# A six-layer cross network on one core: transposing loads in halves, a table for the last biases, and a different split of the first evictions

## The chip, the cores and the metric

The kernel runs on one core of one Trainium2 chip. The metric is the time of one execution on the device in microseconds (us). Three timed runs of the kernel before gave 131.05 us as median, 130.94 as lowest and 131.28 as highest.

## The reference

`x0` is a 4096 x 416 matrix, `ws` holds six 416 x 416 weight matrices and `bs` six bias rows of 416, all in bf16.

```python
def reference(x0, ws, bs):
    x = x0
    for l in range(ws.shape[0]):
        x = x0 * (x @ ws[l] + bs[l]) + x
    return x
```

Each layer is one matrix product over the width, a bias, an elementwise product with `x0` and a sum. In layer 0 `x` is `x0`, so the kernel computes `x0 * (x0 @ ws[0] + bs[0] + 1)` and adds the 1 to the bias beforehand.

## The kernel before, in words

**Layout.** In layers 0 to 4 the activations lie transposed: the width on the 128 partitions, the 4096 rows along the free dimension. The 416 columns are three blocks of 128 (`XM`, blocks `m` or `k`) and a remainder of 32 (`XR`). The rows are two halves `s` of 2048, and each half is four column groups `g` of 512 (`CW`). In the last layer the roles of weights and activations are exchanged, so that its results come out row by row and can be stored as they are.

**Loads.** `load_x0t` (L76) is a DMA that transposes on the way: 512 rows by 384 columns of `x0` go to the three blocks of one column group of `XM[0]`. There are eight. Their order is written out by hand on the queue of SyncE (SP): group 0 at L95, group 1 at L110, `xrem` at L111, groups 2 to 5 at L112 to L115, `xrem` of the second half at L116, groups 6 and 7, then the weights of layer 1 (`load_wm`, L119), the weight rows of the remainder (`load_wr`, L121), the other weights, `X0rows` and a row of last biases, `bLr` (L125). The first weights, the biases and the first weight rows come over the queue of ScalarE (ACT) (L96 to L98), and so does one `xrem` (L275). `xrem` is the 32-column remainder of `x0`, fetched in 64-byte pieces and turned by `x0_rem` (L153): VectorE (DVE) transposes of 32 x 32 blocks, a copy into `XR`, and a copy `XRx` with its halves exchanged.

**Start.** While the first loads are under way TensorE (PE) multiplies a constant tile (`pe_filler`, L148 to L150): three matmuls of 128 columns, nine of 512 and one of 256.

**First layer** (`first_layer`, L226). For each half `s` there are two parts `h` of two column groups. In a part, `full` (L229) issues three matmuls of 512 columns for a block and a column group, 18 in all for the part. In part 0 of half 0 they go group by group: three blocks on group 0, then three on group 1. In half 1 the order is block 0 and 1 on the first group of the part, block 0 and 1 on the second, then block 2 on both, so that the third step already needs the second group. Then `row` (L235) adds the remainder's 32 rows, and the results leave PSUM. `split_first` (L175) empties a block with two engines: ACT takes the first bank with the bias, and DVE the second bank with bias and product in one instruction. `ew_main` (L163) lets ACT take both banks, and DVE multiplies. PSUM is four pairs of banks, handed out in the order of `first_order` (L135): the second block of the next part takes the pair of block 0, and the third takes the pair of block 2.

**Middle layers** (L300). Each of the six tiles (`s`, `m`) of a layer takes 48 matmuls of 32 output rows (L197) and four row matmuls (L203); ACT adds the bias (L166), and DVE multiplies and adds (L171, L172). The results of layer 4 are turned back into rows by DMAs (`xl_dmat` L221, and `scrR` L284 with a POOL copy).

**Last layer** (L329 on). The eight `quads` hold four 128-row pieces each. `mm_q_rows` (L347) multiplies the remainder's rows (L351) and adds the biases by a matmul of one row of ones with a row of `bLr` (L356). `ew_pair` (L360) copies two pieces from PSUM (ACT), multiplies, adds (DVE) and stores on SP. The last two quads go piece by piece (`ew_single`, L371): the sum and store of a piece (`close`) are issued one piece later, after the next piece's product.

Of the kernel before, what the change touches and what calls it, by code (L numbers as in the profile page):

```python
# [9 lines left out]
ACT = mybir.ActivationFunctionType  # L10
ALU = mybir.AluOpType
BF16 = mybir.dt.bfloat16
# [4 lines left out]
def kernel(  # L17
# [16 lines left out]
    CW = 512  # L34
    SW = NG * CW
    NBT = B // P
    LL = L - 1
# [11 lines left out]

    dz = const.tile([P, 2], FP32)  # L50
    warm = const.tile([P, CW], BF16)
    ones = const.tile([P, P], BF16)
    WM = const.tile([P, L, NK, D], BF16)
    WR = const.tile([P, L, D], BF16)
    WD = const.tile([P, L, NG, R], BF16)
    bsb = const.tile([R, D], BF16)
    bT = const.tile([R, D // R, R], BF16)
    bLr = const.tile([P, D], BF16)
# [11 lines left out]
    def col0(s, g):  # L70
        return SW * s + CW * g

    def load_wm(eng, l):
        eng.dma_start(WM[:, l], ws[l, 0:NK * P, :].rearrange("(k p) n -> p k n", p=P))

    def load_x0t(s, g):  # L76
        c0 = col0(s, g)
        nc.sync.dma_start_transpose(out=XM[0][:, :, c0:c0 + CW], in_=x0[c0:c0 + CW, 0:NK * P])


    def load_xrem(eng, s, p0, p1):
# [9 lines left out]
    nc.gpsimd.memset(bsb[:], 0.0)  # L91
    nc.gpsimd.memset(ones[:], 1.0)
    nc.gpsimd.memset(WD[:], 0.0)

    load_x0t(0, 0)  # L95
# [5 lines left out]
    nc.vector.transpose(out=bT[:], in_=bsb.rearrange("p (c r) -> p c r", r=R))  # L101
    for q in range(4):
        nc.gpsimd.tensor_copy(bM[32 * q:32 * q + 32, :, :], bT[:, q:4 * NK:4, 0:L])
    nc.gpsimd.tensor_scalar(out=bM[:, :, 0:1], in0=bM[:, :, 0:1], scalar1=1.0, scalar2=None, op0=ALU.add)
# [1 line left out]
        nc.gpsimd.tensor_copy(bR[32 * g:32 * g + 32, :], bT[:, 4 * NK, 0:L])  # L106
    nc.gpsimd.tensor_scalar(out=bR[:, 0:1], in0=bR[:, 0:1], scalar1=1.0, scalar2=None, op0=ALU.add)
    for g in range(1, NG):
        nc.vector.tensor_copy(WR[32 * g:32 * g + 32, 0, :], WR[0:32, 0, :])
    load_x0t(0, 1)  # L110
    load_xrem(nc.sync, 0, 0, 64)  # L111
    load_x0t(0, 2)  # L112
    load_x0t(0, 3)
    load_x0t(1, 0)
    load_x0t(1, 1)  # L115
    load_xrem(nc.sync, 1, 0, 128)  # L116
    load_x0t(1, 2)
    load_x0t(1, 3)
    load_wm(nc.sync, 1)  # L119
    for g in range(NG):  # L120
        load_wr(nc.sync, g, 1, L)  # L121
    for l in range(2, L):
        load_wm(nc.sync, l)
    nc.sync.dma_start(X0rows[:], x0_v)
    nc.sync.dma_start(bLr[0:P:32, :], bs[LL:LL + 1, :].broadcast_to([NG, D]))  # L125

    def fill_wd(l0, l1):
        for g in range(NG):
# [15 lines left out]
    def pe_filler(n, cols):  # L144
        for i in range(n):
            nc.tensor.matmul(PS[:, 0, 0:cols], lhsT=warm[:, 0:P], rhs=warm[:, 0:cols], start=True, stop=True, skip_group_check=True)  # L146

    pe_filler(3, P)  # L148
    pe_filler(9, CW)
    pe_filler(1, 2 * P)  # L150


    def x0_rem(s, p0, p1, parts):  # L153
# [6 lines left out]
            nc.vector.tensor_copy(XRx[s][64 - a:128 - a, :], XR[0][a:a + 64, CW * s:CW * s + CW])  # L160


    def ew_main(l, s, m, h, pt, cur, nxt):  # L163
        c0 = col0(s, 2 * h)
        t = tpool.tile([P, 2 * CW], BF16, name="t")
        nc.scalar.activation(t[:], pt.rearrange("p a b -> p (a b)"), ACT.Identity, bias=bM[:, m, l:l + 1], scale=1.0)  # L166
        x0c = XM[0][:, m, c0:c0 + 2 * CW]
        if l == 0:
            nc.vector.tensor_tensor(out=nxt[:, m, c0:c0 + 2 * CW], in0=t[:], in1=x0c, op=ALU.mult)  # L169
            return  # L170
        nc.vector.tensor_tensor(out=t[:], in0=t[:], in1=x0c, op=ALU.mult)  # L171
        nc.vector.tensor_tensor(out=nxt[:, m, c0:c0 + 2 * CW], in0=t[:], in1=cur[:, m, c0:c0 + 2 * CW], op=ALU.add)  # L172


    def split_first(s, m, h, pt, nxt):  # L175
        c0 = col0(s, 2 * h)
        t = tpool.tile([P, 2 * CW], BF16, name="t")
        nc.scalar.activation(t[:, 0:CW], pt[:, 0, :], ACT.Identity, bias=bM[:, m, 0:1], scale=1.0)  # L178
        nc.vector.scalar_tensor_tensor(out=nxt[:, m, c0 + CW:c0 + 2 * CW], in0=pt[:, 1, :], scalar=bM[:, m, 0:1],
                                       in1=XM[0][:, m, c0 + CW:c0 + 2 * CW], op0=ALU.add, op1=ALU.mult)  # L180
        nc.vector.tensor_tensor(out=nxt[:, m, c0:c0 + CW], in0=t[:, 0:CW], in1=XM[0][:, m, c0:c0 + CW], op=ALU.mult)

    def ew_rem(l, s, pr, curR, nxtR):
        tr = tpool.tile([P, 2 * CW], BF16, name="t")
# [41 lines left out]
    def first_layer(s):  # L226
        cur, nxt = XM[0], XM[1]

        def full(pt, m, h, gl, first, last):  # L229
            c0 = col0(s, 2 * h + gl)  # L230
            for k in range(NK):
                nc.tensor.matmul(pt[:, gl, :], lhsT=WM[:, 0, k, 128 * m:128 * m + 128], rhs=cur[:, k, c0:c0 + CW],  # L232
                                 start=(first and k == 0), stop=(last and k == NK - 1), skip_group_check=True)
# [9 lines left out]
        for m, gl in ((0, 0), (1, 0), (2, 0), (0, 1), (1, 1), (2, 1)) if s == 0 else ((0, 0), (1, 0), (0, 1), (1, 1), (2, 0), (2, 1)):  # L243
            full(pa[m], m, 0, gl, True, False)
        pb = [two_banks()]
        row(pa[0], 0, 0, 0, False)
        if s == 1:
            row(pb[0], 0, 1, 0, True)
        row(pa[2], 2, 0, 0, False)
        row(pa[1], 1, 0, 1, False)  # L250
        split_first(s, 0, 0, pa[0], nxt)
        if s == 0:
            x0_rem(0, 64, 128, (nc.vector.tensor_copy,))
        for m in (2, 1):
            ew_main(0, s, m, 0, pa[m], cur, nxt)
        pb += [two_banks() for m in range(1, NK)]
        for m, gl in ((0, 0), (1, 0), (2, 0), (0, 1), (1, 1), (2, 1)) if s == 0 else ((0, 0), (1, 0), (0, 1), (1, 1), (2, 0), (2, 1)):
            full(pb[m], m, 1, gl, s == 0 or m > 0, s == 1 and m == 0)
            if s == 1 and (m, gl) == (0, 1):
                ew_main(0, s, 0, 1, pb[0], cur, nxt)  # L260
        if s == 0:
            row(pb[0], 0, 1, 0, False)
            row(pb[1], 1, 1, 0, False)
            row(pb[2], 2, 1, 1, False)
            split_first(s, 0, 1, pb[0], nxt)
            x0_rem(1, 0, 128, (nc.vector.tensor_copy,))
            for m in range(1, NK):
                ew_main(0, s, m, 1, pb[m], cur, nxt)
        else:
            row(pb[1], 1, 1, 0, False)  # L270
            row(pb[2], 2, 1, 1, False)
            rem_first(pb)

    x0_rem(0, 0, 64, (nc.scalar.copy, nc.vector.tensor_copy))
    load_xrem(nc.scalar, 0, 64, 128)  # L275

    def rem_pair(l, cur, curR, nxtR, feeds_last):
        pr2 = two_banks()
# [50 lines left out]
    l = LL  # L329
# [17 lines left out]
    def mm_q_rows(qs, pys, begun):  # L347
        for q, py in zip(qs, pys):
            s, i = quads[q]
            for g in range(NG):  # L350
                nc.tensor.matmul(py[g // 2][:, g % 2, 0:D], lhsT=curR[32 * g:32 * g + 32, CW * s + 128 * i:CW * s + 128 * i + 128],  # L351
                                 rhs=WR[32 * g:32 * g + 32, l, :], start=not (q == begun and g < 2), stop=False,
                                 tile_position=(32 * g, 0), skip_group_check=True)
        for q, py in zip(qs, pys):
            for g in range(NG):
                nc.tensor.matmul(py[g // 2][:, g % 2, 0:D], lhsT=ones[32 * g:32 * g + 1, :],  # L356
                                 rhs=bLr[32 * g:32 * g + 1, :], start=False, stop=(q == begun and g < 2), tile_position=(32 * g, 0),
                                 skip_group_check=True)

    def ew_pair(q, h, py):  # L360
# [4 lines left out]
        o = opool.tile([P, 2, D], BF16, name="o")  # L365
        nc.scalar.copy(tv, py[h][:, :, 0:D])  # L366
        nc.vector.tensor_tensor(out=tv, in0=tv, in1=X0rows[:, b0:b0 + 5:4, :], op=ALU.mult)  # L367
        nc.vector.tensor_tensor(out=o[:], in0=tv, in1=XLrows[:, b0:b0 + 5:4, :], op=ALU.add)  # L368
        nc.sync.dma_start(out_v[:, b0:b0 + 5:4, :], o[:])

    def ew_single(q, g, py):  # L371
        s, i = quads[q]
# [64 lines left out]
```

## Time and profile before

One profiled execution took 130.53 us. Its span, from the first to the last instruction, is 128.7 us; 1.8 us lie around it.

| | before |
|---|---|
| median of three timed runs | 131.05 us |
| profiled execution | 130.53 us |
| its span | 128.7 us |
| PE busy | 122.9 us (95%) |
| DVE busy | 104.2 us (81%) |
| ACT busy | 83.3 us (65%) |
| share of PE in the chain that ended last | 93% |
| the eight `x0` transposing loads, issue to landing | 4.3 to 5.8 us, median 4.8 |

The page gives busy time of each engine first, then the span in 40 slices, the DMA queues, the chain of work that ended last (each instruction followed back to what released it), and the costliest groups of instructions. A row "SPq" is the time in which SP was busy issuing a DMA; the transfer and its landing come later. "PEld" is the load of weights into the array; with back-to-back matmuls its starts show the pace of PE.

### The profile page before, as it was taken

Reading aid. Unit: us, or ns where it says so; the run is one execution under the profiler, and the core shown is the slowest. Engines: PE = TensorE matmul, PEld = TensorE weight load, DVE = VectorE, ACT = ScalarE, POOL = GpSimd, SP = SyncE. Lnnn points to the kernel's source line nnn. Section 1 sums busy time; section 2 is a strip of 40 time slices with the busy share of each in tenths; the row PEclk is TensorE's granted clock in tenths of the full one; section 3 lists DMA queues with packets and bytes.
Section 4 is the critical chain, followed back from the end, with each engine's and each line's share of the span. In section 5 each row is a group of like instructions: output and inputs, shape, how many; then the busy total and the mean of one; then the engine's idle time right before and its main releaser. Section 6 shows DMA issues by size and latency. Waiting matters only on the chain.

```text
span 128.7 us, 3923 instructions
## 1 busy us (share of the span) xinstructions
PE 122.9 (95%) x1677; PEld 54.5 (42%) x1677; DVE 104.2 (81%) x187; ACT 83.3 (65%) x93; POOL 7.0 (5%) x27
## 2 busy tenths in 40 slices
PE   6999999999999999999999999999999999999950
PEld 3343334444434444544444444434444445544420
DVE  1344969457979898989898989898989999999990
ACT  2117358399757759766749666849666877567760
POOL 4250000030000000000000000000000300000000
PEclk9999999999999999999999999999999999999999
DMA  3989989999991000000000000000398899995663
GB/s 94 261 155 222 179 153 277 225 326 333 335 316 30 5 0 8 0 0 5 0 5 0 5 0 5 0 0 5 73 135 185 163 150 234 235 293 176 198 192 103
DMA packets 41973, 16.37 MB, mean 127 GB/s; under 512 B 30778, under 2 KB 41956, under 8 KB 41956
## 3 DMA queue, kind: packets, MB, share of 16 engines
q1 hardware_dynamic: 40456, 15.70, 54.8%
q10 hardware_dynamic: 1500, 0.42, 1.6%
q8 instruction: 13, 0.21, 0.7%
q14 instruction: 4, 0.03, 0.1%
HBM read 6.15 MB, written 3.41 MB: 74 GB/s over the span
## 4 chain that ended last, share of the span: by engine, by line
PE 93%; ACT 2%; DVE 2%; issue 1%; DVEq 0%; ACTq 0%
PE PS L197 49%; PE PS L342 12%; PE PS L232 12%; PE PS L203 5%; PE PS L214 5%; PE PS L146 4%; PE PS L209 2%; PE PS L351 2%; PE PS L239 1%; PE PS L356 1%; DVE t L377 1%; ACT t L166 1%; DVE o L380 1%; ACT t L178 1%; ACT t L376 0%
## 5 line engine op out<-in xcount | busy, mean ns | idle before, releaser
L166 ACT ACTIVATE t<-PS,bM 128x1024 bf16<-128x1024 f32 x57 | 59.1, 1115 | 21.2 <-PE PS L203 21.2
L197 PE MATMUL PS<-XM,WM 128*32 128x512 bf16 x1152 | 65.2, 379 | 0.0
L197 PEld LDWEIGHTS <-WM 128*32 128x32 bf16 x1152 | 29.8, 97 | 33.7 <-issue 5.1
L171 DVE TENSOR_TENSOR t<-t,XM 128x1024 bf16<-128x1024 bf16 x48 | 33.3, 694 | 4.2 <-ACT t L166 4.2
L172 DVE TENSOR_TENSOR XM<-t,XM 128x1024 bf16<-128x1024 bf16 x48 | 33.5, 698 | 3.1
L342 PE MATMUL PS<-WM,XM 128*128 128x416 bf16 x96 | 17.9, 340 | 0.0
L232 PE MATMUL PS<-XM,WM 128*128 128x512 bf16 x72 | 16.9, 385 | 0.2 <-ACT t L166 0.2
L366 ACT CAST t<-PS 128x832 bf16<-128x832 f32 x12 | 10.2, 852 | 5.0 <-PE PS L342 2.3
L342 PEld LDWEIGHTS <-XM 128*128 128x128 bf16 x96 | 8.9, 98 | 8.7 <-issue 2.2
L232 PEld LDWEIGHTS <-WM 128*128 128x128 bf16 x72 | 6.9, 99 | 10.1 <-issue 2.8
L214 PE MATMUL PS<-XM,WM 128*32 128x512 bf16 x120 | 8.2, 379 | 0.0
L185 ACT ACTIVATE t<-PS,bR 128x512 bf16<-128x512 f32 x10 | 6.8, 694 | 2.0 <-POOL WD L129 2.0
L368 DVE TENSOR_TENSOR o<-t,XLrows 128x832 bf16<-128x832 bf16 x12 | 7.1, 592 | 0.5
L203 PE MATMUL PS<-XR,WR 32*128 32x512 bf16 x96 | 7.3, 379 | 0.0
L169 DVE TENSOR_TENSOR XM<-t,XM 128x1024 bf16<-128x1024 bf16 x9 | 5.9, 688 | 1.5 <-ACT t L166 1.5
L367 DVE TENSOR_TENSOR t<-t,X0rows 128x832 bf16<-128x832 bf16 x12 | 7.0, 584 | 0.0
L146 PE MATMUL PS<-warm 128*128 128x512 bf16 (+2 forms) x13 | 4.6, 535 | 1.0 <-DVE warm L88 1.0
L178 ACT ACTIVATE t<-PS,bM 128x512 bf16<-128x512 f32 x3 | 2.1, 687 | 5.3 <-PE PS L239 5.3
L285 POOL COPY XLrows<-scrR 128x512 bf16<-128x512 bf16 x2 | 1.3, 666 | 72.7 <-DMA scrR<-XR 72.7
L157 DVE STREAM_TRANSPOSE xrt<-xrem 64x256 bf16<-64x256 bf16 (+2 forms) x4 | 2.2, 562 | 3.5 <-DMA xrem<-in_x_dram 3.5
L376 ACT CAST t<-PS 128x416 bf16<-128x416 f32 x8 | 4.0, 506 | 1.0 <-PE PS L342 0.8
L214 PEld LDWEIGHTS <-WM 128*32 128x32 bf16 x120 | 3.2, 97 | 3.2
(40 smaller groups left out, 48.1 us busy)
## 6 DMA issues: line engine op xcount, KB each, us to landing
X0rows<-in_x_dram SPq DMA_DIRECT2D x1, 3328.0 KB, 15.3
out_dram<-o SPq DMA_DIRECT2D x12, 208.0 KB, 2.6
WM<-in_ws_dram SPq DMA_DIRECT2D x5, 312.0 KB, 6.5
out_dram<-o SPq DMA_DIRECT2D x8, 104.0 KB, 1.7
WR<-in_ws_dram SPq DMA_DIRECT2D x4, 130.0 KB, 6.0
WM<-in_ws_dram ACTq DMA_DIRECT2D x1, 312.0 KB
XM<-in_x_dram SPq DMA_TRANSPOSE x8, 4.8
xrem<-in_x_dram SPq DMA_DIRECT2D x1, 128.0 KB, 4.4
```

The source lines that it names most:

```text
L146: nc.tensor.matmul(PS[:, 0, 0:cols], lhsT=warm[:, 0:P], rhs=warm[:, 0:cols], start=True, stop=True, skip_group_check=True)
L166: nc.scalar.activation(t[:], pt.rearrange("p a b -> p (a b)"), ACT.Identity, bias=bM[:, m, l:l + 1], scale=1.0)
L171: nc.vector.tensor_tensor(out=t[:], in0=t[:], in1=x0c, op=ALU.mult)
L172: nc.vector.tensor_tensor(out=nxt[:, m, c0:c0 + 2 * CW], in0=t[:], in1=cur[:, m, c0:c0 + 2 * CW], op=ALU.add)
L197: nc.tensor.matmul(pts[g // 2][32 * q:32 * q + 32, g % 2, :], lhsT=WM[:, l, k, 128 * m + 32 * q:128 * m + 32 * q + 32], rhs=cur[:, k, c0:c ...
L203: nc.tensor.matmul(pts[g // 2][:, g % 2, :], lhsT=WR[32 * g:32 * g + 32, l, 128 * m:128 * m + 128], rhs=curR[32 * g:32 * g + 32, CW * s:CW ...
L214: nc.tensor.matmul(pr[32 * g:32 * g + 32, :], lhsT=WM[:, l, k, NK * P:D], rhs=cur[:, k, c0:c0 + CW], start=False, stop=(k == NK - 1), tile ...
L232: nc.tensor.matmul(pt[:, gl, :], lhsT=WM[:, 0, k, 128 * m:128 * m + 128], rhs=cur[:, k, c0:c0 + CW], start=(first and k == 0), stop=(last ...
L342: nc.tensor.matmul(py[g // 2][:, g % 2, 0:D], lhsT=cur[:, k, q_cols(q, g)], rhs=WM[:, l, k, :], start=(first and k == 0), stop=((not first ...
L366: nc.scalar.copy(tv, py[h][:, :, 0:D])
L367: nc.vector.tensor_tensor(out=tv, in0=tv, in1=X0rows[:, b0:b0 + 5:4, :], op=ALU.mult)
L368: nc.vector.tensor_tensor(out=o[:], in0=tv, in1=XLrows[:, b0:b0 + 5:4, :], op=ALU.add)
```

## The change

1. `load_x0t` fetches 256 rows, so there are sixteen loads in place of eight. On SP's queue the two halves of a group follow each other. The `xrem` that went over ACT's queue is now on SP's, behind group 3. `bLr` and its load are gone.
2. PE's fillers are three of 128 columns, seven of 512 and one of 128.
3. The first column group of half 0 is multiplied in two halves of 256 columns: nine matmuls on the first, nine on the second.
4. In part 0 of half 0, blocks 0 and 2 are both emptied by `split_first`; block 1 is copied by ACT. The DVE products of the first banks are issued after both splits, and that of block 1 after the turning of `xrem`, whose copy is shared between ACT and DVE.
5. The last biases come from `bsb`, whose rows 0 to 5 are the six biases; POOL copies them to the other three groups of 32 partitions. `pick[1]` has ones in row 5 of each group of 32, so a matmul with K = 32 picks the last bias.
6. The first four quads of the last layer collect four pieces in `o4` and store them with one DMA each; at the end, the sums of some pieces are issued earlier (`keep`).

```diff
-    def load_x0t(s, g):
-        c0 = col0(s, g)
-        nc.sync.dma_start_transpose(out=XM[0][:, :, c0:c0 + CW], in_=x0[c0:c0 + CW, 0:NK * P])
+    def load_x0t(s, g, a):
+        c0 = col0(s, g) + HW * a
+        nc.sync.dma_start_transpose(out=XM[0][:, :, c0:c0 + HW], in_=x0[c0:c0 + HW, 0:NK * P])
...
-    nc.gpsimd.memset(ones[:], 1.0)
+    nc.vector.memset(pick[0][:], 0.0)
+    nc.vector.memset(pick[0][:, LL:P:R], 1.0)
+    nc.vector.transpose(out=pick[1][:], in_=pick[0][:])
...
+    for g in range(1, NG):
+        nc.gpsimd.tensor_copy(bsb[32 * g:32 * g + 32, :], bsb[0:R, :])
...
-    load_x0t(0, 1)
+    load_x0t(0, 0, 1)
+    load_x0t(0, 1, 0)
+    load_x0t(0, 1, 1)
     load_xrem(nc.sync, 0, 0, 64)
-    load_x0t(0, 2)
-    load_x0t(0, 3)
-    load_x0t(1, 0)
-    load_x0t(1, 1)
+    load_x0t(0, 2, 0)
+    load_x0t(0, 2, 1)
+    load_x0t(0, 3, 0)
+    load_x0t(0, 3, 1)
+    load_xrem(nc.sync, 0, 64, 128)
+    load_x0t(1, 0, 0)
...
-    nc.sync.dma_start(bLr[0:P:32, :], bs[LL:LL + 1, :].broadcast_to([NG, D]))
...
-    pe_filler(9, CW)
-    pe_filler(1, 2 * P)
+    pe_filler(7, CW)
+    pe_filler(1, P)
...
+        if s == 0:
+            for part in range(2):
+                for m in range(NK):
+                    full(pa[m], m, 0, 0, True, False, part)
...
-        split_first(s, 0, 0, pa[0], nxt)
         if s == 0:
-            x0_rem(0, 64, 128, (nc.vector.tensor_copy,))
-        for m in (2, 1):
-            ew_main(0, s, m, 0, pa[m], cur, nxt)
+            closing = [split_first(s, 0, 0, pa[0], nxt)]
+            closing.append(split_first(s, 2, 0, pa[2], nxt))
+            t1 = ew_copy(0, 1, pa[1])
+            for close in closing:
+                close()
+            x0_rem(0, 64, 128, (nc.scalar.copy, nc.vector.tensor_copy))
+            nc.vector.tensor_tensor(out=nxt[:, 1, 0:2 * CW], in0=t1, in1=XM[0][:, 1, 0:2 * CW], op=ALU.mult)
...
-    load_xrem(nc.scalar, 0, 64, 128)
...
-                nc.tensor.matmul(py[g // 2][:, g % 2, 0:D], lhsT=ones[32 * g:32 * g + 1, :],
-                                 rhs=bLr[32 * g:32 * g + 1, :], start=False, stop=(q == begun and g < 2), tile_position=(32 * g, 0),
+                nc.tensor.matmul(py[g // 2][:, g % 2, 0:D], lhsT=pick[1][32 * g:32 * g + 32, :],
+                                 rhs=bsb[32 * g:32 * g + 32, :], start=False, stop=(q == begun and g < 2), tile_position=(32 * g, 0),
...
+        if q >= 4:
+            nc.sync.dma_start(out_v[:, b0:b0 + 5:4, :], o)
+        elif h == 1:
+            nc.sync.dma_start(out_v[:, b0 - 8:b0 + 5:4, :], o4[q][:])
...
-            close = ew_single(q, g, py)
-            if pending:
-                pending.pop()()
-            pending.append(close)
-    pending.pop()()
+            pending.append(ew_single(q, g, py))
+            keep = 0 if (q, g) in ((NQ - 2, NG - 1), (NQ - 1, 0), (NQ - 1, NG - 1)) else 1
+            while len(pending) > keep:
+                pending.pop(0)()
```

More of the change, by code (lines that the diff above doesn't have):

```diff
@@ L34 @@
     CW = 512
+    HW = CW // 2
     SW = NG * CW
@@ L51 @@
     warm = const.tile([P, CW], BF16)
-    ones = const.tile([P, P], BF16)
+    pick = [const.tile([P, P], BF16, name=f"pick{i}") for i in range(2)]
     WM = const.tile([P, L, NK, D], BF16)
@@ L55 @@
     WD = const.tile([P, L, NG, R], BF16)
-    bsb = const.tile([R, D], BF16)
+    bsb = const.tile([P, D], BF16)
     bT = const.tile([R, D // R, R], BF16)
-    bLr = const.tile([P, D], BF16)
     bM = const.tile([P, NK, L], FP32)
@@ L90 @@
     nc.vector.memset(dz[:], 0.0)
-    nc.gpsimd.memset(bsb[:], 0.0)
-    nc.gpsimd.memset(ones[:], 1.0)
+    nc.gpsimd.memset(bsb[0:R, :], 0.0)
+    nc.vector.memset(pick[0][:], 0.0)
+    nc.vector.memset(pick[0][:, LL:P:R], 1.0)
+    nc.vector.transpose(out=pick[1][:], in_=pick[0][:])
     nc.gpsimd.memset(WD[:], 0.0)
-    load_x0t(0, 0)
+    load_x0t(0, 0, 0)
     load_wm(nc.scalar, 0)
@@ L99 @@
     nc.scalar.activation(dz[:, 1:2], dz[:, 0:1], ACT.Identity, bias=dz[:, 0:1], scale=1.0)
-    nc.vector.transpose(out=bT[:], in_=bsb.rearrange("p (c r) -> p c r", r=R))
+    nc.vector.transpose(out=bT[:], in_=bsb[0:R, :].rearrange("p (c r) -> p c r", r=R))
     for q in range(4):
@@ L108 @@
     for g in range(1, NG):
+        nc.gpsimd.tensor_copy(bsb[32 * g:32 * g + 32, :], bsb[0:R, :])
+    for g in range(1, NG):
         nc.vector.tensor_copy(WR[32 * g:32 * g + 32, 0, :], WR[0:32, 0, :])
-    load_x0t(0, 1)
+    load_x0t(0, 0, 1)
+    load_x0t(0, 1, 0)
+    load_x0t(0, 1, 1)
     load_xrem(nc.sync, 0, 0, 64)
-    load_x0t(0, 2)
-    load_x0t(0, 3)
-    load_x0t(1, 0)
-    load_x0t(1, 1)
+    load_x0t(0, 2, 0)
[4 more added lines that the diff above has]
+    load_x0t(1, 0, 0)
+    load_x0t(1, 0, 1)
+    load_x0t(1, 1, 0)
+    load_x0t(1, 1, 1)
     load_xrem(nc.sync, 1, 0, 128)
-    load_x0t(1, 2)
-    load_x0t(1, 3)
+    load_x0t(1, 2, 0)
+    load_x0t(1, 2, 1)
+    load_x0t(1, 3, 0)
+    load_x0t(1, 3, 1)
     load_wm(nc.sync, 1)
@@ L160, in x0_rem, with ew_copy @@
             nc.vector.tensor_copy(XRx[s][64 - a:128 - a, :], XR[0][a:a + 64, CW * s:CW * s + CW])
+    def ew_copy(l, m, pt):
+        t = tpool.tile([P, 2 * CW], BF16, name="t")
+        nc.scalar.activation(t[:], pt.rearrange("p a b -> p (a b)"), ACT.Identity, bias=bM[:, m, l:l + 1], scale=1.0)
+        return t[:]
     def ew_main(l, s, m, h, pt, cur, nxt):
         c0 = col0(s, 2 * h)
-        t = tpool.tile([P, 2 * CW], BF16, name="t")
-        nc.scalar.activation(t[:], pt.rearrange("p a b -> p (a b)"), ACT.Identity, bias=bM[:, m, l:l + 1], scale=1.0)
+        t = ew_copy(l, m, pt)
         x0c = XM[0][:, m, c0:c0 + 2 * CW]
         if l == 0:
-            nc.vector.tensor_tensor(out=nxt[:, m, c0:c0 + 2 * CW], in0=t[:], in1=x0c, op=ALU.mult)
+            nc.vector.tensor_tensor(out=nxt[:, m, c0:c0 + 2 * CW], in0=t, in1=x0c, op=ALU.mult)
             return
-        nc.vector.tensor_tensor(out=t[:], in0=t[:], in1=x0c, op=ALU.mult)
-        nc.vector.tensor_tensor(out=nxt[:, m, c0:c0 + 2 * CW], in0=t[:], in1=cur[:, m, c0:c0 + 2 * CW], op=ALU.add)
+        nc.vector.tensor_tensor(out=t, in0=t, in1=x0c, op=ALU.mult)
+        nc.vector.tensor_tensor(out=nxt[:, m, c0:c0 + 2 * CW], in0=t, in1=cur[:, m, c0:c0 + 2 * CW], op=ALU.add)
     def split_first(s, m, h, pt, nxt):
@@ L180, in split_first @@
                                        in1=XM[0][:, m, c0 + CW:c0 + 2 * CW], op0=ALU.add, op1=ALU.mult)
-        nc.vector.tensor_tensor(out=nxt[:, m, c0:c0 + CW], in0=t[:, 0:CW], in1=XM[0][:, m, c0:c0 + CW], op=ALU.mult)
+        return lambda: nc.vector.tensor_tensor(out=nxt[:, m, c0:c0 + CW], in0=t[:, 0:CW], in1=XM[0][:, m, c0:c0 + CW], op=ALU.mult)
     def ew_rem(l, s, pr, curR, nxtR):
@@ L227, in first_layer, with full @@
         cur, nxt = XM[0], XM[1]
-        def full(pt, m, h, gl, first, last):
-            c0 = col0(s, 2 * h + gl)
+        def full(pt, m, h, gl, first, last, part=None):
+            a, n = (0, CW) if part is None else (HW * part, HW)
+            c0 = col0(s, 2 * h + gl) + a
             for k in range(NK):
-                nc.tensor.matmul(pt[:, gl, :], lhsT=WM[:, 0, k, 128 * m:128 * m + 128], rhs=cur[:, k, c0:c0 + CW],
-                                 start=(first and k == 0), stop=(last and k == NK - 1), skip_group_check=True)
+                nc.tensor.matmul(pt[:, gl, a:a + n], lhsT=WM[:, 0, k, 128 * m:128 * m + 128], rhs=cur[:, k, c0:c0 + n],
+                                 start=(first and k == 0 and part != 1), stop=(last and k == NK - 1), skip_group_check=True)
         def row(pt, m, h, swapped, first):
@@ L242, in first_layer @@
         pa = [two_banks() for m in range(NK)]
-        for m, gl in ((0, 0), (1, 0), (2, 0), (0, 1), (1, 1), (2, 1)) if s == 0 else ((0, 0), (1, 0), (0, 1), (1, 1), (2, 0), (2, 1)):
+        if s == 0:
+            for part in range(2):
+                for m in range(NK):
+                    full(pa[m], m, 0, 0, True, False, part)
+        for m, gl in ((0, 1), (1, 1), (2, 1)) if s == 0 else ((0, 0), (1, 0), (0, 1), (1, 1), (2, 0), (2, 1)):
             full(pa[m], m, 0, gl, True, False)
@@ L250, in first_layer @@
         row(pa[1], 1, 0, 1, False)
-        split_first(s, 0, 0, pa[0], nxt)
         if s == 0:
-            x0_rem(0, 64, 128, (nc.vector.tensor_copy,))
-        for m in (2, 1):
-            ew_main(0, s, m, 0, pa[m], cur, nxt)
+            closing = [split_first(s, 0, 0, pa[0], nxt)]
[5 more added lines that the diff above has]
+            nc.vector.tensor_tensor(out=nxt[:, 1, 0:2 * CW], in0=t1, in1=XM[0][:, 1, 0:2 * CW], op=ALU.mult)
+        else:
+            split_first(s, 0, 0, pa[0], nxt)()
+            for m in (2, 1):
+                ew_main(0, s, m, 0, pa[m], cur, nxt)
         pb += [two_banks() for m in range(1, NK)]
@@ L264, in first_layer @@
             row(pb[2], 2, 1, 1, False)
-            split_first(s, 0, 1, pb[0], nxt)
+            split_first(s, 0, 1, pb[0], nxt)()
             x0_rem(1, 0, 128, (nc.vector.tensor_copy,))
@@ L355, in mm_q_rows @@
             for g in range(NG):
-                nc.tensor.matmul(py[g // 2][:, g % 2, 0:D], lhsT=ones[32 * g:32 * g + 1, :],
-                                 rhs=bLr[32 * g:32 * g + 1, :], start=False, stop=(q == begun and g < 2), tile_position=(32 * g, 0),
+                nc.tensor.matmul(py[g // 2][:, g % 2, 0:D], lhsT=pick[1][32 * g:32 * g + 32, :],
+                                 rhs=bsb[32 * g:32 * g + 32, :], start=False, stop=(q == begun and g < 2), tile_position=(32 * g, 0),
                                  skip_group_check=True)
+    o4 = [big.tile([P, NG, D], BF16, name=f"o4_{q}") for q in range(4)]
     def ew_pair(q, h, py):
@@ L364, in ew_pair @@
         tv = t[:, 0:2 * D].rearrange("p (a d) -> p a d", a=2)
-        o = opool.tile([P, 2, D], BF16, name="o")
+        o = o4[q][:, 2 * h:2 * h + 2, :] if q < 4 else opool.tile([P, 2, D], BF16, name="o")[:]
         nc.scalar.copy(tv, py[h][:, :, 0:D])
         nc.vector.tensor_tensor(out=tv, in0=tv, in1=X0rows[:, b0:b0 + 5:4, :], op=ALU.mult)
-        nc.vector.tensor_tensor(out=o[:], in0=tv, in1=XLrows[:, b0:b0 + 5:4, :], op=ALU.add)
-        nc.sync.dma_start(out_v[:, b0:b0 + 5:4, :], o[:])
+        nc.vector.tensor_tensor(out=o, in0=tv, in1=XLrows[:, b0:b0 + 5:4, :], op=ALU.add)
+        if q >= 4:
+            nc.sync.dma_start(out_v[:, b0:b0 + 5:4, :], o)
+        elif h == 1:
+            nc.sync.dma_start(out_v[:, b0 - 8:b0 + 5:4, :], o4[q][:])
     def ew_single(q, g, py):
```

## The prediction

> **What bounds the kernel now.** I read the page's busy rows, then the chain that ended last, then the waits, and last the timeline of SP.
>
> ```profile
> PE 122.9 (95%) x1677; PEld 54.5 (42%) x1677; DVE 104.2 (81%) x187; ACT 83.3 (65%) x93; POOL 7.0 (5%) x27
> PE 93%; ACT 2%; DVE 2%; issue 1%; DVEq 0%; ACTq 0%
> ```
>
> PE is the bound: busy for 95% of the span and 93% of the chain. A gain must start PE's real work earlier, remove a gap, or shorten what follows its last matmul. The chain in order of time shows the stage that the change touches:
>
> ```profile
> 1.04 4.61 PE PS L146 x13
> 5.65 4.29 PE PS L232 x18
> ...
> 19.93 4.14 PE PS L232 x18
> ...
> 26.23 2.59 PE PS L197 x48
> ```
>
> Fillers end where the first real matmul starts (5.52 on the timeline of PE); the trace has the first load's last landing event at 5.48. The waits show one gap of PE in the first layer:
>
> ```profile
> PE PS L232 <- ACT t L166: 0.2, 1, 0.2
> ```
>
> The third thing to see is SP's queue, by narrow windows of its timeline (start, us, what):
>
> ```profile
> 0.71 1.40 SPq L78 DMA_TRANSPOSE XM<-in_x_dram  x1
> 4.80 0.67 SPq L83 DMA_DIRECT2D xrem<-in_x_dram  x1
> 5.52 1.97 SPq L78 DMA_TRANSPOSE XM<-in_x_dram  x1
> 9.10 4.08 SPq L78 DMA_TRANSPOSE XM<-in_x_dram  x2
> 13.22 0.59 SPq L83 DMA_DIRECT2D xrem<-in_x_dram  x1
> 13.85 3.12 SPq L78 DMA_TRANSPOSE XM<-in_x_dram  x1
> 17.02 1.42 SPq L78 DMA_TRANSPOSE XM<-in_x_dram  x1
> L284 SPq DMA_TRANSPOSE scrR<-XR x2: 1216/1216/1217, 96.9 to 98.2; - x2
> L221 SPq DMA_TRANSPOSE XLrows<-XM x6: 1867/2232/3118, 91.0 to 107.6; - x6
> ```
>
> SP issues without a pause from 0.72 to 18.44: the stream of loads is bound by its issue. And it has no slack: group 7 lands at 21.27 (trace), and PE needs it for its third step of the part that starts at 19.93, six matmuls of 0.216 later, at 21.22. So PE and the stream of loads are two bounds of equal length over the first 21 us. A gain at the start is kept only if the last load lands earlier too.
>
> **The change part by part**, on the profiled execution (130.53 us: span 128.7 and 1.8 around it). The three timed runs' median is 131.05, 0.52 above it; I add differences to the median.
>
> *Fillers and first group.* Two matmuls of 512 and 128 columns less: 2 x 0.427 + 0.107 = 0.96 us, so real work could start at about 4.5. But PE's pace is that of these weight loads:
>
> ```profile
> 4.81 0.15 PEld L146 LDWEIGHTS <-warm 128*128 128x128 bf16 x1 [0.28 <-issue]
> 5.90 0.15 PEld L232 LDWEIGHTS <-WM 128*128 128x128 bf16 x1 [0.28 <-issue]
> 6.33 0.10 PEld L232 LDWEIGHTS <-WM 128*128 128x128 bf16 x1 [0.28 <-issue]
> ```
>
> One per 0.427 us until 6.33, and 0.216 from there. Real work moved ahead of 6.33 runs at half pace: 0.96 us at 0.427 a matmul is 2.25 matmuls, and these cost 2.25 x 0.216 = 0.49 later. So the gain is 0.5 us. The page's clock row (9 throughout) doesn't show this. [...] Does the first half land by 4.5? A whole load took 4.76 us from issue to landing; the half saves at most 0.70 of issue and about 0.68 of transfer (768 packets at the trace's 225 per 0.2 us): 3.4 to 4.2 us, landing between 4.1 and 4.9. About right, and up to 0.4 late.
>
> *Third block on two engines.* ACT took 0.69 for a first bank and 1.05 for a whole block; the third block was free at 12.06. Now ACT needs 2 x 0.69 and DVE 2 x 0.75 from 10.39: free at 11.9, when PE arrives. The 0.2 us go. Queued behind on DVE are two products and the turning of `xrem`; next late is that `xrem`.
>
> *Tail.* DVE's product at 124.81 stood ready on ACT's side at 124.64 and waited for a sum. Sums of earlier pieces now go ahead, one of them into DVE's idle 0.07 us before 123.09, so at most 0.17 is to be had; I take 0.1.
>
> *At nothing.* The bias matmuls have as many columns (0.35 for eight, L356). Three new DVE instructions lie in its 3.2 us of waiting for `bsb`. POOL's three copies (0.3 to 0.7 each by its rows L129 and L285) delay `WD`, needed at 24.4 and ready at 8.7. Four larger stores for eight lie before the eight single stores that end the kernel. If a cover fails, the cost is the row itself, at most 1 us.
>
> *The loads.* Sixteen issues for eight, and a third `xrem` on SP. What does the issue of a half cost? The trace shows none. By proportion it is 0.70, half of 1.40. At the other end stands scrR, 512 packets in 1.22: a line through it and the load's 1536 in 1.40 gives 1.26 for 768. Its source is SBUF, not DRAM, so neither row decides. I take the load's own row less a slope: XLrows (2048 packets) and scrR differ by 1.87 - 1.22 = 0.65 for 1536 packets, so 768 fewer take off 0.33: **1.08**. The longer issues (1.97, 3.12) end when the load ahead has drained, and halves leave room for that. Each DMA also waits for the landing of the eighth DMA before it, which by then was issued 9 us ago against landings of 4.3 to 5.8: no cost. With 0.045 between issues, 16 x 1.125 + 3 x (0.63 + 0.045) = 20.0, so the last issue ends at 20.7 instead of 18.44. The last load landed 2.83 after its issue; a half has 0.68 less to move and less ahead of it (0.3): 1.9. It lands at 22.6, **1.3 us later than before**, and PE waits for it. This wait swallows the 0.5 and the 0.2. Layer 1's weights are issued at 20.8 instead of 18.48; they took 6.2 us to land with the queue full, so 27.0 at the latest, against a need at 26.23 + 1.3. Covered by 0.5.
>
> [...]
>
> Sum: +1.3 - 0.1 = **+1.2 us, 132.3 us** on the median's scale.
>
> **Rivals.** (1) *The halves keep up.* If a half is issued in 0.95 or less, the last issue ends by 0.72 + 16 x 0.995 + 2.0 = 18.6, the landing follows by 20.5, and PE keeps its gains: 0.5 + 0.2 + 0.1 = 0.8, so 130.25 (129.9 to 130.7). For it: equal source, equal shape, and two halves in flight can hide each other's start, which the trace shows as thin stretches of packets at 9.0 to 9.6 and 13.5 to 14.0. Against it: scrR's 1.22. (2) *Issue has a floor.* At 1.26 the last issue ends at 23.6 and lands at 25.5: +4.2 - 0.1, 135.1 us. `xrem`, the groups and layer 1's weights would each be late on the way, absorbed by the last. For it: a third of the packets cost 1.22. (3) *A draw*: at 1.0 the landing is at 21.3 as before, and gain and loss cancel: 131.0. That the first half doesn't do what it says (its landing after 4.5) costs at most 0.2 at half pace, inside these ranges.
>
> So the forecast ends slower, and rival 1 is the other side, decided at 0.95 to 1.0 us a half.
>
> **Chances.** Forecast (0.4 to 2.9 us slower, a half at 1.0 to 1.17) 0.36; floor 0.20; keep up 0.34; draw 0.10. This kernel's measurement can tell about 0.3%, 0.4 us. So faster 0.34, same 0.10, slower 0.56. The forecast's own range is 131.5 to 134.0; with both rivals it is 130.0 to 135.3.
>
> **What would show it.** The half's row on SP: 1.08 right, 0.95 or less rival 1, 1.2 or more rival 2. Waits of PE at L251 for XM loads, above all in half 1, and none of 0.2 for ACT. L197's first start: 26.23 now, 27.5 by my sum, 25.5 by rival 1, 30 by rival 2. DVE's last sum 0.1 nearer to PE's end. Wrong would be: no waits for loads, or waits for `WM` of layer 1.

## The result and the profile after

By the ratio, the changed kernel takes 137.5 us where the kernel before takes 131.1: 1.0489 times as long (95% interval 1.0457 to 1.0521), about 6.4 us. The forecast was 132.3; its own range ended at 134.0, and with both rivals at 135.3. Of its four runs two took 137.12 and 137.77 us, and the other two, 139.43 (the profiled one) and 140.52, had a lower mean granted clock (0.981 and 0.975 against 0.993 and 1.000) and are left out of the ratio, so 1.7 us of what the page shows belong to the clock (below).

First the page's busy rows, then two of its rows of 40 slices (3.4 us each): PE's busy tenths and PE's granted clock.

```profile
PE 124.7 (91%) x1684; PEld 55.7 (40%) x1684; DVE 105.0 (76%) x192; ACT 83.5 (61%) x94; POOL 8.3 (6%) x29
...
PE   6877768669999999999999999999999999999970
...
PEclk9999999986999999999999999999999999999997
```

PE has nearly as much busy time as before (124.7 against 122.9) in a span that is 8.9 us longer, and its slices are below 9 only in the first nine, 31 us, and at the very end. The loss lies in the first layer. The clock's row drops in the ninth and tenth slice. The chain that ended last is of no help here: on this page it can be followed back over 6% of the span and stops in the tail. So the next view is the waits (engine, tile, line, what ended the wait; us in total, times, longest):

```profile
PEld L251 <- DMA XM<-in_x_dram: 8.2, 7, 2.4
PE PS L251 <- DMA XM<-in_x_dram: 7.2, 8, 1.9
```

Before, PE's one wait for data in this layer was 0.2 us for ACT. That wait is gone, as forecast; in its place stand eight waits for loads of `x0`, 7.2 us together, and one of 0.25 us for the turned remainder. PE's timeline shows that the longest is the last (start, us, instruction; in brackets the idle time ahead and what ended it):

```profile
5.08 2.58 PE L251 MATMUL PS<-XM,WM 128*128 128x256 bf16 x18 [0.39 <-DMA XM<-in_x_dram]
8.42 2.12 PE L251 MATMUL PS<-XM,WM 128*128 128x512 bf16 x9 [0.75 <-DMA XM<-in_x_dram]
10.78 0.61 PE L258 MATMUL PS<-XR,WR 32*128 32x512 bf16 x4 [0.25 <-DVE XR L171]
...
12.18 2.12 PE L251 MATMUL PS<-XM,WM 128*128 128x512 bf16 x9 [0.71 <-DMA XM<-in_x_dram]
15.18 2.12 PE L251 MATMUL PS<-XM,WM 128*128 128x512 bf16 x9 [0.88 <-DMA XM<-in_x_dram]
...
28.82 4.24 PE L251 MATMUL PS<-XM,WM 128*128 128x512 bf16 x12 [1.95 <-DMA XM<-in_x_dram]
...
35.21 2.77 PE L214 MATMUL PS<-XM,WM 128*32 128x512 bf16 x48
```

PE starts its real work at 5.08 instead of 5.52, and has lost this 0.44 by the second column group (8.42 against 7.84). L214 is what was L197, the middle layers' first line. The same view of the kernel before has it here:

```profile
26.06 2.76 PE L197 MATMUL PS<-XM,WM 128*32 128x512 bf16 x48
```

So 35.21 stands against 26.06, and the middle layers start 9.15 us late. (The prediction's 26.23 is the chain's figure, which counts a piece from the end of the one before it.) From there to its last matmul PE takes 98.0 us in both kernels, and what lies behind that matmul is 0.3 us shorter, which gives the 8.9. The row of SP's issues (shortest, median, longest in ns; first and last start) and SP's timeline say why:

```profile
L78 SPq DMA_TRANSPOSE XM<-in_x_dram x16: 1268/1282/2811, 0.7 to 24.5; - x16
```

```profile
18.97 6.80 SPq L78 DMA_TRANSPOSE XM<-in_x_dram  x4
25.81 0.58 SPq L74 DMA_DIRECT2D WM<-in_ws_dram  x1
```

A half takes 1.28 us to issue, not 1.08, and never less than 1.27. The last issue ends at 25.77 instead of 18.44, and the last load lands at 28.77 (trace) instead of 21.27: 7.5 us later. The rest of the 9.15 is the clock, by stretches of the trace (stretch, length, busy time and instructions of each engine, then the clock, the DMA share and GB/s):

```profile
26.90:28.80 1.90, 0.00 (x0) 0.00 (x0) 1.19 (x2) 0.24 (x1) 0.00 (x0) 1.00 0.70 164
28.80:30.00 1.20, 1.18 (x6) 0.60 (x7) 0.00 (x0) 0.32 (x1) 0.00 (x0) 0.98 1.17 283
30.00:33.30 3.30, 3.30 (x12) 0.89 (x10) 0.69 (x1) 0.79 (x1) 1.30 (x4) 0.50 1.15 246
33.30:36.00 2.70, 2.70 (x52) 1.31 (x52) 0.43 (x1) 1.38 (x2) 0.00 (x0) 0.99 1.11 326
```

PE stood still for 1.95 us, began, and then ran at half rate from 29.95 to 33.36 (the trace's record): 3.41 us at half rate are 1.7 lost. 7.5 + 1.7 = 9.2.

### The profile page after: what moved, and what is told of

The parts are those of the page before. It is cut to its first block, busy times and chain, and to the rows that moved or that the text cites. A ratio compares the mean times of both kernels' runs of the same rounds, so it can differ in the third digit from the quotient of the medians.

```text
span 137.6 us, 3940 instructions
## 1 busy us (share of the span) xinstructions
PE 124.7 (91%) x1684; PEld 55.7 (40%) x1684; DVE 105.0 (76%) x192; ACT 83.5 (61%) x94; POOL 8.3 (6%) x29
## 3 DMA queue, kind: packets, MB, share of 16 engines
HBM read 6.15 MB, written 3.41 MB: 69 GB/s over the span
## 5 line engine op out<-in xcount | busy, mean ns | idle before, releaser
L178 ACT ACTIVATE t<-PS,bM 128x1024 bf16<-128x1024 f32 x56 | 58.2, 1114 | 23.8 <-PE PS L220 21.3
L214 PE MATMUL PS<-XM,WM 128*32 128x512 bf16 x1152 | 65.2, 380 | 0.0
L214 PEld LDWEIGHTS <-WM 128*32 128x32 bf16 x1152 | 29.8, 97 | 33.7 <-issue 5.1
L189 DVE TENSOR_TENSOR XM<-t,XM 128x1024 bf16<-128x1024 bf16 x48 | 33.5, 699 | 3.1
L251 PE MATMUL PS<-XM,WM 128*128 128x512 bf16 (+1 forms) x81 | 18.9, 386 | 7.2 <-DMA XM<-in_x_dram 7.2
L251 PEld LDWEIGHTS <-WM 128*128 128x128 bf16 x81 | 8.0, 104 | 17.2 <-DMA XM<-in_x_dram 8.2
L170 DVE STREAM_TRANSPOSE xrt<-xrem 64x256 bf16<-64x256 bf16 (+1 forms) x5 | 2.2, 477 | 9.2 <-DMA xrem<-in_x_dram 9.2
L186 DVE TENSOR_TENSOR XM<-t,XM 128x1024 bf16<-128x1024 bf16 x7 | 4.7, 690 | 3.9 <-ACT t L178 3.9
L171 ACT COPY XR<-xrt 64x256 bf16<-64x256 bf16 x2 | 1.2, 619 | 8.9 <-DVE xrt L170 8.9
L195 ACT ACTIVATE t<-PS,bM 128x512 bf16<-128x512 f32 x4 | 2.6, 686 | 5.5 <-PE PS L258 5.5
L159 PE MATMUL PS<-warm 128*128 128x512 bf16 (+1 forms) x11 | 3.7, 511 | 1.0 <-DVE warm L88 1.0
```

The source lines that it names most:

```text
L214: nc.tensor.matmul(pts[g // 2][32 * q:32 * q + 32, g % 2, :], lhsT=WM[:, l, k, 128 * m + 32 * q:128 * m + 32 * q + 32], rhs=cur[:, k, c0:c ...
L251: nc.tensor.matmul(pt[:, gl, a:a + n], lhsT=WM[:, 0, k, 128 * m:128 * m + 128], rhs=cur[:, k, c0:c0 + n], start=(first and k == 0 and part ...
```

## The experiments

The theory after the result: an issue of a transposing load has a floor that hardly depends on its rows, so the number of loads sets the end of the stream. The rivals: the other parts of the change carry the loss; the issues are slow because something ahead in the queues holds them, and not for a floor; the clock carries it. Each run stands beside runs of the kernel before on the same chip, and the ratios are to those.

### Which part: the half loads alone, and everything else alone

The first kernel is the one before with only the loads cut in two; the second is the changed one with eight whole loads, the old fillers, an undivided first group and the third `xrem` back on ACT.

```diff
# halves only
-        c0 = col0(s, g)
-        nc.sync.dma_start_transpose(out=XM[0][:, :, c0:c0 + CW], in_=x0[c0:c0 + CW, 0:NK * P])
+        for a in range(2):
+            c0 = col0(s, g) + 256 * a
+            nc.sync.dma_start_transpose(out=XM[0][:, :, c0:c0 + 256], in_=x0[c0:c0 + 256, 0:NK * P])
...
# the rest alone, against the changed kernel
-        c0 = col0(s, g) + HW * a
-        nc.sync.dma_start_transpose(out=XM[0][:, :, c0:c0 + HW], in_=x0[c0:c0 + HW, 0:NK * P])
+        if a == 1:
+            return
+        c0 = col0(s, g)
+        nc.sync.dma_start_transpose(out=XM[0][:, :, c0:c0 + CW], in_=x0[c0:c0 + CW, 0:NK * P])
...
-    pe_filler(7, CW)
-    pe_filler(1, P)
+    pe_filler(9, CW)
+    pe_filler(1, 2 * P)
```

> The kernel before with sixteen half loads and nothing else of the change: SP's order, xrem on ACT's queue, nine fillers and whole matmuls on group 0 stay. Theory (the issue): a half costs SP 1.28 us in the changed kernel against 1.41 for a whole one, so the number of loads sets the stream; the last issue ends at 24 to 25.5 instead of 18.44, and the time is 136 to 138.5 us, nearly all of the change's loss. Rival (the rest of the change costs: xrem moved to SP, the split evictions, the new order on DVE): at most 133 us.

> The changed kernel with the eight whole loads, the xrem on ACT's queue, the fillers and the undivided first group of before, so all of the change but its loads and start. Theory (the issue): the 0.2 us gap of PE behind ACT goes and the tail gives at most 0.1, so 130.7 to 131.1 us. Rival (the rest costs): 133 us or more. If the tail's new order of sums does nothing, the last sum still ends 2.8 us after ACT begins the last quad.

The halves alone: 137.01 us, 1.0508 (1.0486 to 1.0529). The rest alone: 130.42 us, 0.999 (0.9978 to 1.0003), beside 130.56 for the kernel before. So the loads carry the whole loss, and all the rest together is worth nothing that can be measured. In the halves alone no clock falls, so its terms add up without that: the last issue ends at 24.78 (6.3 later than before), the last load lands at 27.50 (6.2 later), and the middle layers start at 32.31 (6.3 later than 26.06). SP's issues and the last wait of PE:

```profile
L79 SPq DMA_TRANSPOSE XM<-in_x_dram x16: 1262/1282/2692, 0.7 to 23.5; - x16
```

```profile
27.55 2.76 PE L233 MATMUL PS<-XM,WM 128*128 128x512 bf16 x12 [1.74 <-DMA XM<-in_x_dram]
...
32.31 1.90 PE L198 MATMUL PS<-XM,WM 128*32 128x512 bf16 x32
```

In the rest alone, PE's timeline shows what became of the 0.2 us that ACT no longer takes:

```profile
10.18 2.10 PE L252 MATMUL PS<-XM,WM 128*128 128x512 bf16 x9
12.71 2.10 PE L252 MATMUL PS<-XM,WM 128*128 128x512 bf16 x9 [0.42 <-DMA XM<-in_x_dram]
```

PE goes from the third block's first group into a wait of 0.42 us for the next column group. So the gap for ACT had stood where, without it, PE waits for a load that isn't there yet.

### Is it a floor? Loads of other sizes

Three kernels cut only some loads: group 0 in two halves, with the fillers and the divided multiplication of the change (nine loads); group 0 in four loads of 128 rows (eleven); all of half 1 in halves (twelve). A fourth goes the other way and loads half 1 in two loads of 1024 rows (six loads).

```diff
# quarters of group 0 (the others: 256 for group 0; 256 for s == 1)
+        n = P if (s, g) == (0, 0) else CW
+        for a in range(0, CW, n):
+            c0 = col0(s, g) + a
+            nc.sync.dma_start_transpose(out=XM[0][:, :, c0:c0 + n], in_=x0[c0:c0 + n, 0:NK * P])
...
# two loads of 1024 rows in half 1
+        n = CW if s == 0 else 2 * CW
+        if n > CW and g % 2 == 1:
+            return
```

> The kernel before with only group 0 in two halves, with the changed kernel's fillers and its two-part multiplication of group 0; seven whole loads follow. Theory (the issue): one more issue of 1.3 us, of which up to 1.1 may go into the wait of 2.57 that the second load's issue held before; the last load lands 0.2 to 1.3 later, and since PE has no slack there the time is 131.2 to 132.3 us although PE starts 0.4 us earlier. Rival (halves do no harm): 130.5 us.

> The kernel before with group 0 in four loads of 128 rows, the other seven whole. Theory (a floor of 1.15 us and 0.13 for 256 rows): each quarter is issued in 1.20 to 1.25 us; three more issues than before, the first real matmul waits for the fourth at about 5.0 + 4.2 = 9 us instead of 5.5, and the time is about 134.5 us. Rival (the issue grows with the rows, and halves are dear for another reason): 0.4 to 0.7 us each and at most 132 us.

> The kernel before with halves only for the four groups of half 1: twelve loads. Theory (the count of loads behind a saturated queue): SP reaches half 1 at 9.1 as before, then eight issues of 1.325, one of them held to 2.7, and a remainder's 0.64: the last ends at 21.7 instead of 18.44, and the time is 133.5 to 134.5 us. Rival (only the loads of half 0 matter, since PE starts there): at most 131.5 us.

> The kernel before with the four loads of half 1 joined to two of 1024 rows; six loads in all. Theory (a fixed part of about 1.15 us for each issue and 0.13 for 256 rows): a load of 1024 rows takes 1.7 us when nothing holds it, and two together end SP's loads about 1 us earlier than 18.44. Group 4 then lands with group 5, about 1.7 us later than its 14.40, and PE waits up to 0.7 for it: 131 to 132 us. Rival (the issue grows with the rows): 2.8 us and more for each load, the same end of the issues, and 132 us or more.

| kernel | loads | us | ratio (95%) | last issue ends | last load lands |
|---|---|---|---|---|---|
| before | 8 | 130.6 | 1 | 18.44 | 21.27 |
| 1024 rows in half 1 | 6 | 131.58 | 1.0098 (1.0073-1.0122) | 18.25 | 20.35 |
| group 0 in halves | 9 | 131.58 | 1.0091 (1.0072-1.011) | 19.08 | 21.62 |
| group 0 in quarters | 11 | 133.57 | 1.0233 (1.0217-1.0249) | 21.33 | 23.88 |
| half 1 in halves | 12 | 134.21 | 1.0276 (1.0262-1.029) | 21.56 | 24.52 |
| halves only | 16 | 137.01 | 1.0508 (1.0486-1.0529) | 24.78 | 27.50 |

Group 0 in halves and half 1 in halves came out as expected (131.2 to 132.3 and 133.5 to 134.5).

The quarters decide for a floor. Their issues took 1.29, 1.24, 1.29 and 1.26 us: a load of 128 rows costs as much as one of 256, and a whole one that nothing holds costs 1.40.

```profile
0.71 1.29 SPq L80 DMA_TRANSPOSE XM<-in_x_dram  x1
2.06 1.24 SPq L80 DMA_TRANSPOSE XM<-in_x_dram  x1
3.35 1.29 SPq L80 DMA_TRANSPOSE XM<-in_x_dram  x1
4.69 1.26 SPq L80 DMA_TRANSPOSE XM<-in_x_dram  x1
L80 SPq DMA_TRANSPOSE XM<-in_x_dram x11: 1244/1489/3103, 0.7 to 19.8; - x11
```

The first issue of a run has nothing ahead of it in the queue, and so can't be held by anything there. It took 1.29 us with 128 rows, 1.32 to 1.35 with 256 and 1.36 to 1.41 with 512, over all profiled runs. Of the changed kernel's sixteen issues fourteen took 1.27 to 1.36, much the same. This speaks against the rival that something ahead makes the issues slow; that holds only for the longest ones (below).

```profile
1.04 4.61 PE L148 MATMUL PS<-warm 128*128 128x128 bf16 x13 [1.04 <-DVE warm L90]
7.33 2.10 PE L234 MATMUL PS<-XM,WM 128*128 128x512 bf16 x9 [1.68 <-DMA XM<-in_x_dram]
```

Here PE starts 1.8 us later than before, since group 0 is whole only at 7.20. I had expected about 9, and 134.5 us where 133.57 were measured.

The 1024-row loads went against the theory. I had expected the stream to end about a microsecond sooner, with issues of 1.7; SP was busy for 3.91 us with the first and for this long with the second:

```profile
13.88 4.37 SPq L81 DMA_TRANSPOSE XM<-in_x_dram  x1
```

Those are 2.0 and 2.2 us for each 512 rows, about what whole loads take in the stream of the kernel before (eight issues in 16.03 us, 2.0 each, though 1.40 would do). So the stream before was not bound by issue work, as the prediction had read it: SP was mostly held by the packets ahead, which move 512 rows in some 2 us. In the trace of the kernel before, each of the six issues that took longer than 1.42 ends within some 0.2 us of the start of the last packet ahead of it. Two halves cost 2 x 1.325 = 2.65 (the median of 1.28 and 0.045 between issues), more than those 2.0. This is where the bound passes from the transfers to the issues. The time, 131.58, lies in the 131 to 132 expected, but not for the reason given: PE waits only 0.23 us for these loads, the middle layers start 0.4 late, and 0.5 more lies behind the last matmul.

### What holds an issue beyond its floor

In the changed kernel one issue of a half took 2.81 us. It stands right behind the `xrem` of half 1, 2048 pieces of 64 bytes; before, the issue in this place took 3.12. The kernel of halves only was run without that load (the remainder of half 1 is zeros, so that part of the result is left out).

```diff
-    load_xrem(nc.sync, 1, 0, 128)
+    nc.gpsimd.memset(xrem[1][:], 0.0)
```

> The kernel of sixteen half loads alone, without the load of the remainder's 32 columns of half 1 (zeros are put there instead). Theory (a load behind 64-byte pieces is held, on top of the 1.28): the issue of 2.69 becomes 1.28 and 0.64 of the piece load's own issue goes, the last issue ends at 22.7 instead of 24.78, and the time falls by about 2.0 to 135.0 us. Rival (the long issue has another cause): the 2.7 stays, and 136.4 us.

135.39 us, 1.0367 (1.034 to 1.0393): by the ratios 1.8 us less than with that load. The long issue in this place is gone, and every issue but the last took 1.26 to 1.34. The last, which put the end of the stream at 23.74 where 22.7 was expected, is this one:

```profile
21.48 2.25 SPq L79 DMA_TRANSPOSE XM<-in_x_dram  x1
```

A 16 KB packet of the queue "instruction" starts at 21.39 and takes 1.29 us. The changed kernel's page counts these packets:

```profile
q8 instruction: 13, 0.21, 0.6%
```

Before, such a packet came at 21.78, after the last load had landed. In the changed kernel it came at 26.08 (0.94 us), with the last loads on their way, and the last of these landed 3.0 us after its issue ended instead of the 1.9 forecast. Such a packet stood beside the last loads in the halves only too (24.84; 2.7 us) and in one of the two changed kernels below (25.62; 3.5 us); in the other it came at 22.36, beside an issue of 2.22, and there the last load landed after 1.9. That fits. But no run moved the packets, and the first twelve halves of the changed kernel landed 2.4 to 3.1 us after their issue with no such packet near, so the packets' part in the late landing is not shown.

Then two sizes between: loads of 512, 512, six times 448 and 384 rows (nine), and of 512, 512 and eight times 384 (ten). The idea was that a load is held while more than some 1500 packets are ahead of it; loads a little smaller than 512 rows would slip under that and end the stream sooner. The 448-row loads were also run with the rest of the change.

```diff
-    load_x0t(0, 2)
-    load_x0t(0, 3)
...
+    load_x0t(1024, 448)
+    load_x0t(1472, 448)
...
+    load_x0t(3264, 448)
+    load_x0t(3712, 384)
```

The ten loads replace the same lines with `load_x0t(512, 512)`, `load_x0t(1024, 384)` and so on in steps of 384 rows.

> The kernel before with nine loads of other sizes: 512, 512, six of 448 rows and 384; SP's order and all else stay. Theory (an issue ends after its own 1.3 to 1.4 us, or when no more than about 1500 packets still wait to start, whichever is later; a load of 512 rows is 1536 packets): loads a little under that size are no longer held until the load ahead has drained, so they are issued in 1.4 to 1.8 us instead of 2.0, and SP is through with the loads at 17.0 to 17.8 instead of 18.44 in spite of one load more. PE has no other wait to lose than at half 1, so the time is 130.2 to 131.0 us. Rival (the count of loads alone decides): one load more, as in the run with group 0 in halves, and 131.5 us.

> The same nine loads, with the evictions, the bias table, the stores and the tail of the changed kernel (all but its loads, fillers and divided first group). Theory (PE's start and the stream were two bounds of equal length): with the stream ahead, the 0.2 us of the third block's eviction becomes a gain instead of a wait for group 3: 130.0 to 130.4 us, 0.2 below the same loads without it. Rival: no difference between the two.

> The kernel before with ten loads: 512, 512 and eight of 384 rows. Theory (as for the 448 rows): 1152 packets, never held, 1.34 to 1.4 us each except behind the remainder's load; SP is through with the loads at about 17.8 to 18.3, and the time is 130.4 to 131.2 us. Rival (the count of loads alone decides): two loads more, 132.3 us.

All three fell short: 132.78 us, 1.0112 (1.0086 to 1.0138); with the rest of the change 132.38, 1.0105 (1.0066 to 1.0144); the 384-row loads 133.24, 1.015 (1.0128 to 1.0171). The 448-row issues took 1.42 at the least, but the others 1.47 to 2.77, and the last ended at 20.05 where 17.0 to 17.8 was expected. A bound on the packets ahead is not the whole rule. Counted in the traces, 1465 to 1566 packets were issued and not yet started when a held whole load's issue ended in the kernel before, and 1504 and 1657 with the 1024-row loads: near the bound. But the 448-row issues behind them ended only at 1068 to 1439, short of it. What holds those stays open. Whether the rest of the change is worth its 0.2 us here can't be told either, since the two ratios' intervals overlap. Besides, a column group now needs two loads:

```profile
11.78 2.12 PE L232 MATMUL PS<-XM,WM 128*128 128x512 bf16 x9 [1.48 <-DMA XM<-in_x_dram]
14.19 2.10 PE L232 MATMUL PS<-XM,WM 128*128 128x512 bf16 x9 [0.30 <-DMA XM<-in_x_dram]
```

### The clock

To see whether the fall of the clock carries the loss, the changed kernel was run with constant matmuls (into banks that the next step starts afresh) in four of PE's waits, and once more as it is.

```diff
+    def feed(dst, n):
+        for i in range(n):
+            nc.tensor.matmul(dst, lhsT=warm[:, 0:P], rhs=warm[:, 0:CW], start=True, stop=True, skip_group_check=True)
...
+            if (m, gl) == (0, 1):
+                feed(pa[1][:, 1, :], 3 if s == 0 else 6)
...
+            if (m, gl) == (0, 1):
+                feed(pb[1][:, 1, :], 3 if s == 0 else 8)
```

> The changed kernel, with matmuls of the constant tile put into the four longest waits of PE for loads (three in each part of half 0, six and eight in half 1), into a bank that the next step overwrites; the result is unchanged. Theory (the wait lets PE's clock fall): no stretch at half pace between 10 and 130 us, every run's clock at 0.99 or more, and all runs within 1 us around 137.2. Rival (the low clock comes from outside the kernel): some runs still show 0.975 to 0.981 and 139 to 140.5 us.

> The changed kernel once more, beside the others. Theory (the clock falls when the windows in which PE waited lie so): some runs again show a lower mean clock and 139 us or more, the others lie at 136.8 to 137.8. Rival (it was a disturbance of that chip): all runs within 1 us.

Fed, five runs took 137.5 to 138.3 us, 1.0553 (1.0531 to 1.0574), and the profiled one shows no fall. Again as it is: 1.053 (1.0475 to 1.0585), with two of six runs at 139.5 and a fall of 3.41 us, after a wait of 3.31, in the profiled one; the other four, 137.48 to 137.64, are 1.048 times the kernel before. PE's last load step and the start of the middle layers, fed and then unfed again:

```profile
28.46 2.75 PE L255 MATMUL PS<-XM,WM 128*128 128x512 bf16 x12
...
33.21 1.04 PE L214 MATMUL PS<-XM,WM 128*32 128x512 bf16 x16
```

```profile
27.46 5.75 PE L251 MATMUL PS<-XM,WM 128*128 128x512 bf16 x18 [3.31 <-DMA XM<-in_x_dram]
...
35.20 1.04 PE L214 MATMUL PS<-XM,WM 128*32 128x512 bf16 x16
```

Eighteen such matmuls took 4.04 us where the clock was whole (the same step with 448-row loads); here they take 5.75. With PE kept busy the step runs at full rate, the middle layers start 2.0 us sooner than in the profiled runs with a fall, and yet the kernel isn't faster than an undisturbed run of the changed one. So the fall costs its 1.7 us where it happens, and is no part of the 6.4. That feeding prevents it is likely but not shown: five fed runs had none, against four of ten unfed ones with a low clock.

## Why the prediction was wrong

**The step that failed** is the price of a half: "I take the load's own row less a slope ... **1.08**". It measured 1.282 in the median, and a quarter cost the same. The row that was set aside because "its source is SBUF, not DRAM", scrR's 1.22 for 512 packets, was the near one; the line through it and the whole load gave 1.26. The slope had come from XLrows and scrR, and did not carry over: from 384 to 1536 packets a load's first issue grew by about 0.1 us, where the slope says 0.49. XLrows' rows probably contain a wait. Four of its six issues ended with 1509 to 1529 packets not yet started, the first of them with nothing ahead of it, so at least that one may have waited for its own 2048 packets. This is read from the counts, and no run tested it. If so, it was a difference of two rows of which one contains a wait, and that is no price of a packet. The reading that the stream was "bound by its issue" failed too, as the 1024-row loads showed; it became true only with the halves.

**The sum, mended.** Forecast: the last issue ends at 20.7. Sixteen halves at 0.20 more are 3.2; the half behind the 64-byte pieces was held for 1.53 beyond its floor, two others for 0.33: 20.7 + 3.2 + 1.53 + 0.33 = 25.76, measured 25.77. "Halves leave room" for the long issues to end was wrong for the longest of them. The landing followed 3.0 us later instead of 1.9: 28.8. So of 6.2 us between forecast and measured landing, 3.2 are the floor, 1.9 the held issues, and 1.1 the last transfer, whose cause stays open.

**The rivals.** The floor was named, with the right mechanism and 1.26 as its price, and had 0.20; its 135.1 was too low because it too left out the held issue (1.5) and the late landing. "The halves keep up" fell: it needed 0.95, and no half took less than 1.26.

**The start.** "Real work could start at about 4.5", the first half landing "between 4.1 and 4.9": it landed at 5.04 (4.83 with group 0 alone in halves), PE started at 5.08. A little late, and without effect, as the text had it: the next load's wait swallowed it.

**Third block on two engines.** "The 0.2 us go": they went, and a wait for a load of 0.42 took their place in the rest alone. "Next late is that `xrem`" was wrong; the column group was. (The changed kernel's 0.25 us for a turned remainder come earlier, in the first part, and so belong to the first `xrem`.)

**Tail.** "I take 0.1": from ACT's first copy of the last quad to the start of DVE's last sum it was 2.83 us before (122.55 to 125.38) and 2.80 after (131.69 to 134.49): nothing. The last store is issued 0.16 to 0.18 us after DVE's last sum in the five profiled runs with the new tail and 0.19 to 0.61 after it in the nine with the old one, but 0.19 in the kernel before itself; whether the new order wins anything beside other loads is not shown.

**At nothing**: the bias table, POOL's copies and the larger stores were costed at nothing, and the rest alone agrees (0.999).

**Right**: the direction, slower; PE waits for loads above all in half 1, and no wait of 0.2 for ACT. The test named, "1.2 or more rival 2", is what the profile shows.

## What to carry to other kernels

Before cutting a transfer up, compare the issue of the smallest piece with the time in which its packets move. Here 512 rows move in some 2.0 us and cost 1.40 to issue as one load, 2.65 as two: with halves the issues are the bound, and every load beyond the eight cost 0.8 to 1.2 us by the ratios of the table above. What the smaller piece saved at the start here, 0.44 us, was waited off at the next load. And when the rows of a profile give two prices for an operation that it doesn't show, the row of an instruction that waits for nothing is worth more than one of the same kind with a wait inside.

## What was not expected of the hardware

**The issue of a transposing load is nearly flat in its rows**: with nothing ahead in the queue 1.29 us for 128, 1.32 to 1.35 for 256 and 1.36 to 1.41 for 512. That is about 0.1 us more for four times the rows. The shortest of all were 1.24 for 128, 1.26 for 256, 1.35 for 384, 1.42 for 448 and 1.34 for 512.

**PE's clock changed at different times for the same work.** The trace's record of its release to full rate lies between 3.98 and 7.07 us in the profiled runs, though all start their fillers at 1.03 to 1.05 us; two with the same fillers and the same nine loads had 3.98 and 6.99 (their first eighteen matmuls of 512 columns took 4.04 and 4.73). It fell again, for 3.41 us, after a wait of 1.95 us in one run, 3.31 in another, and did not after one of 1.74. The fall after 1.95 us began at 29.95, 1.13 us after PE had gone on at 28.82. What sets these times is not shown.
